# Two attention blocks on one core: block A's projections by quarters of x with all six weight sets for each, and a new written-out loop order

## Chip, core and metric

The kernel runs on one core of a Trainium2 chip. The metric is the device time of one execution in microseconds, as the median of the runs shown. All arithmetic is float32 (the TensorE operands are mostly stored as pairs of a rounded high part and a remainder).

## What is computed

Two attention blocks take inputs of the same shape, x of 2048 x 640, a joint projection weight of 640 x 1920 and an output weight of 640 x 640, with 32 heads of 20. Block A is a local attention: each position looks at 8 positions, itself and every second one before it. Block B is full attention. The outputs stand side by side.

```python
def _A_ref(x, wqkv, wo):
    qkv = (x @ wqkv).reshape(B, S, 3, H, Dh).transpose(2, 0, 3, 1, 4)
    q, k, v = qkv[0], qkv[1], qkv[2]
    idx = pos[:, None] - (jnp.arange(8) * 2)[None, :]      # masked where < 0
    logits = jnp.einsum("bhsd,bhswd->bhsw", q, kg) * scale
    attn = _softmax(jnp.where(mask, logits, -1e9), axis=-1)
    o = jnp.einsum("bhsw,bhswd->bhsd", attn, vg)
    return o.transpose(0, 2, 1, 3).reshape(B, S, D) @ wo
def _B_ref(x, wqkv, wo):
    scores = jnp.einsum("bhqd,bhkd->bhqk", q, k) * (Dh ** -0.5)
    o = jnp.einsum("bhqk,bhkd->bhqd", _softmax(scores, axis=-1), v)
    return o.transpose(0, 2, 1, 3).reshape(B, S, D) @ wo
return jnp.concatenate([_A_ref(...), _B_ref(...)], axis=-1)
```

## The kernel before

**Engines and helpers.** Everything is emitted in program order through a small wrapper (`InOrder`, lines 52 to 66), which is why all instructions of the profile carry line 65. Each engine therefore works through its own list strictly in the order in which the program was written. The profile is read by tile names: `ps_st` is the whole PSUM of eight banks, `w` a tile of a weight set, `akv` a tile of gathered keys or values of block A, `mx` the running maxima of block B, `last` and `big` two pools of larger tiles, `ro` a finished block of 128 x 320 results on its way to memory, `misc` a result of block B on its way to normalization.

**Start.** A short warm-up of TensorE on an identity matrix (lines 216 to 229) comes while the first weights and rows arrive: two transposes and 28 small matmuls in several tile shapes (`in_tiles`). Then come block B's query and key projections (40 groups of 15 matmuls), then its value projection, mixed with the first 80 pairs of matmuls of the maxima pass. From there the main loop runs.

**The main loop** (lines 969 to 1109) follows a written-out order, the string `ORDER`. It is a list of tokens, and the digits behind a letter are the PSUM banks it writes:

- `V`: one of 512 steps of block B's second product (`b_pv`, four matmuls of 128 x 32 by 512, each run as two). A V also begins a new tick (`begin`), on which everything with a due time is issued: DMAs, splits, DVE's pieces of A's softmax.
- `S`, `M`, `Y`: two matmuls of 60 or 62 rows by 512 columns, one on each half of the array's rows. In S both are scores of block B that ScalarE exponentiates. In M both are of the maxima pass, which DVE reduces. A Y has one of each.
- `F`: one step of a projection, two matmuls of 64 rows by 320 columns on the two halves of the array. 30 F tokens make one group of two blocks of 128 x 320.

The work behind F is the list `f_left` (lines 971 to 973): 48 groups of block A's projections (`a_group`), 16 of A's output projection (`oa_group`), 12 of B's (`ob_group`). Groups that `ORDER` doesn't reach are done behind the loop, by `leftover`, with 30 matmuls over all 128 rows instead of 60 over 64.

**A's projections before.** The six weight sets (two of queries, two of keys, two of values, each 640 x 320) pass over x in two halves. `f_left` runs over 12 values of `si`: sets 0 to 5 with the quarters 0 and 1 of x, then the six again with the quarters 2 and 3. Each value has four groups. The first six are loaded raw and split into high part and remainder (`set_pieces`: ScalarE copies, GpSimd subtracts), and the finished tiles are stored to a DRAM tile `w_d`. The second six are read back from it ready-made (`set_again`, two DMAs of 800 KB). A set is asked for at the beginning of the first group of the set before it. The `w` pool holds two sets.

**A's attention** (`a_attention`, with `a_scores`, `a_softmax`, `a_values`) is done by GpSimd on `akv` tiles that DMAs gather from the projected rows in DRAM. It goes by 16 tiles of 128 rows. A tile's scores need its rows of keys, its values its rows of values, and `a_rows` counts both. The function `pump` issues these operations in step with a model of the loop's clock (`COST`, `AHEAD`). Finished tiles are transposed by DVE, pass through DRAM (`a_turn`, `a_back`) and set `ready_a`, without which no group of A's output projection is started.

Of the kernel before, what the change touches and what calls it, by code (L numbers as in the profile page):

```python
# [21 lines left out]
KC = 5  # L22
# [26 lines left out]
NA = 12  # L49
# [20 lines left out]
def attention_pair(ctx, tc, xa, wqk_a, wv_a, wo_a, xb, wqk_b, wv_b, wo_b, oa, ob):  # L70
# [149 lines left out]
    for _ in range(2):  # L220
        pe.transpose(psb[:, 7, :128], ident, ident)

    def in_tiles(rows, cols):
        for r in range(128 // rows):
            for c in range(128 // cols):
                pe.matmul(psb[c * cols:(c + 1) * cols, 5 + r, :128], ident[r * rows:(r + 1) * rows, c * cols:(c + 1) * cols],
                          ident[r * rows:(r + 1) * rows], start=True, stop=True)
    for size in ((64, 128), (64, 32), (64, 128), (64, 32), (64, 128), (128, 32), (64, 128)):
        in_tiles(*size)
# [207 lines left out]
    def normalize(raw, u, then):  # L437
# [15 lines left out]
        t = (1, 4, 5, 8, 10, 11) if then else (1, 5, 6, 10, 12, 14)  # L453
# [57 lines left out]
    def a_softmax(t):  # L511
# [7 lines left out]
        job(soft_jobs, 5, lambda: dve.tensor_reduce(m[:, 0], L.rearrange("p o h -> p h o"), AX.X, ALU.max))  # L519
# [12 lines left out]
        job(soft_jobs, 5, lambda: dve.reciprocal(m[:, 0], m[:, 0]))  # L532
# [23 lines left out]
    def a_attention():  # L556
# [5 lines left out]
        while now[0] < begun + 3:  # L562
            yield False
# [134 lines left out]

    w_d = dr.tile([NA // 2, 2, 128, KC * 320], F32, name="w_d")

# [49 lines left out]
    def xa_pieces(n):  # L750
        def piece(k):
# [3 lines left out]
            after(5, split_piece, k, raw)  # L755
# [215 lines left out]
    f_left = [lambda ns, si=si, n=n, a=a: a_group(si, n, a, ns) for si in range(NA) for n in range(si // 6 * 2, si // 6 * 2 + 2) for a in range(2)]  # L971
# [23 lines left out]
    def pump():  # L995
# [10 lines left out]
        "Y01Y52Y40S36Y41Y35Y72Y60V4Y15S73Y26VY10Y75Y63VY12Y05Y67VY52F01FY36FFFY75FFY32FFFY67FFFFY25FY63VY56FFY73FFF"  # L1006
        "Y25FFY67FFFS32FFFM5FFY73VY61Y25Y37VS12Y06Y53VY61Y23Y70VY36Y51Y27VY03S51Y62VY35Y07Y12VY67Y30Y51VF36Y27FY50FFF"
        "FFY21FFY75FFFY20FFY71VY01Y72VFY75Y12VY05FY12FFY47FFS50FFY21FFFY74FFY05FFFM1V7Y30Y56Y41VY25Y36S04VY26Y31Y50V"
        "Y64S13Y52VY61S02Y43VY65Y13Y02VY41F56FFY02FFY43FFFY10FFY24FFFFM0FS32VY31FY42FFFFY30FFFY41FFY23FFFY40FFM1VY06"
        "Y35Y42VY56Y30S14VY52Y06Y31VM5Y42Y30VY41F65FFY32FFY04FFFY31FFY02FFFY34FFM0VVY04FY23FFFFM0FFY24VY02FFY41FFFY73"  # L1010
        "FFFY40F12FFY37FFFY60FFY45Y37FFFFFY46FFY35Y07V4VY07Y65FFFFFY03FFY76FFFY50FFY73FFFM5VY12Y70Y65VY03Y27Y16VY32"
# [172 lines left out]
```

## Time and profile before

| | |
|---|---|
| median of 3 runs | 1691.92 us (1691.88 to 1693.69) |
| the profiled execution, its own time | 1690.99 us |
| its span, first to last instruction | 1689.2 us |
| PE busy | 1680.1 us (99%) |
| DVE busy | 1360.6 us (81%) |
| ACT busy | 1244.8 us (74%) |
| POOL busy | 938.7 us (56%) |
| DMA, share of the 16 engines' span | 52.6% in the main queue |

PE is TensorE, PEld its weight loads, DVE is VectorE, ACT is ScalarE, POOL is GpSimd, SP is SyncE, which issues nearly all DMAs. The slices of the page cut the span into 40 pieces of 42.2 us, with a digit for the busy tenths of each. Busy times of PE contain matmuls that overlap or wait in the pipeline, so that the 99% don't say how dense the work is; that is read from the starts of successive matmuls.

### The profile page before, as it was taken

Reading aid. Unit: us, or ns where it says so; the run is one execution under the profiler, and the core shown is the slowest. Engines: PE = TensorE matmul, PEld = TensorE weight load, DVE = VectorE, ACT = ScalarE, POOL = GpSimd, SP = SyncE. Lnnn points to the kernel's source line nnn. Section 1 sums busy time; section 2 is a strip of 40 time slices with the busy share of each in tenths; the row PEclk is TensorE's granted clock in tenths of the full one; section 3 lists DMA queues with packets and bytes.
Section 4 is the critical chain, followed back from the end, with each engine's and each line's share of the span. In section 5 each row is a group of like instructions: output and inputs, shape, how many; then the busy total and the mean of one; then the engine's idle time right before and its main releaser. Section 6 shows DMA issues by size and latency. Waiting matters only on the chain.

```text
span 1689.2 us, 37961 instructions
## 1 busy us (share of the span) xinstructions
PE 1680.1 (99%) x14312; PEld 1012.0 (60%) x14312; DVE 1360.6 (81%) x2102; ACT 1244.8 (74%) x2425; POOL 938.7 (56%) x853
## 2 busy tenths in 40 slices
PE   9999999999999999999999999999999999999999
PEld 7888974665655565555565655345454445544669
DVE  4336998998998999899888989889998989888201
ACT  4221158787788778877878788988889888888881
POOL 0000121010179059999999999999999991022420
PEclk9999999999999999999999999999999999999999
DMA  7675553233375355767676765767667652222312
GB/s 252 226 228 175 160 159 108 68 107 101 125 228 164 113 187 189 235 195 223 185 241 187 221 212 159 191 178 214 163 181 191 198 157 72 66 78 67 95 54 90
DMA packets 208071, 272.20 MB, mean 161 GB/s; under 512 B 94860, under 2 KB 126488, under 8 KB 207640
## 3 DMA queue, kind: packets, MB, share of 16 engines
q1 hardware_dynamic: 207252, 269.04, 52.6%
q8 instruction: 112, 1.84, 0.5%
q10 hardware_dynamic: 636, 0.74, 0.1%
q14 instruction: 71, 0.58, 0.1%
HBM read 194.97 MB, written 73.82 MB: 159 GB/s over the span
## 4 chain that ended last, share of the span: by engine, by line
PE 90%; DVE 6%; ACT 1%; POOL 1%; issue 1%; DMA 0%; POOLq 0%; SPq 0%; ACTq 0%; DVEq 0%
PE ps_st L65 90%; DVE mx L65 6%; ACT big L65 1%; POOL akv L65 1%; ACT last L65 0%; DMA akv<-va_d 0%; DVE am L65 0%; ACT misc L65 0%; POOL big L65 0%; POOL misc L65 0%; DVE mxt L65 0%; ACT stg L65 0%; POOL am L65 0%; DVE stg L65 0%; DVE last L65 0%
## 5 line engine op out<-in xcount | busy, mean ns | idle before, releaser
L65 DVE TENSOR_REDUCE mx<-ps_st 128x1 f32<-128x512 f32 (+1 forms) x1811 | 1262.4, 752 | 129.1 <-PE ps_st L65 119.0
L65 ACT ACTIVATE big<-ps_st 128x512 f32<-128x512 f32 x1172 | 636.9, 619 | 130.2 <-PE ps_st L65 117.9
L65 PE MATMUL ps_st<-big,last 60*128 60x512 f32 x2048 | 693.0, 427 | 0.8 <-DVE mx L65 0.2
L65 PE MATMUL ps_st<-last,big 62*128 62x512 f32 x2048 | 666.2, 422 | 3.6 <-ACT big L65 1.2
L65 PEld LDWEIGHTS ps_st<-last,big 62*128 62x128 f32 x2048 | 315.0, 185 | 393.7 <-DVE mx L65 156.0
L65 ACT ACTIVATE last<-ps_st 128x512 f32<-128x512 f32 x876 | 474.5, 621 | 74.8 <-PE ps_st L65 65.7
L65 PE MATMUL ps_st<-w,big 64*128 64x320 f32 (+1 forms) x4560 | 491.1, 307 | 0.0
L65 PEld LDWEIGHTS ps_st<-w,big 64*128 64x128 f32 (+1 forms) x4560 | 427.5, 186 | 33.5 <-issue 6.5
L65 PE MATMUL ps_st<-big,vb 128*32 128x512 f32 x2344 | 384.8, 603 | 0.0
L65 PEld LDWEIGHTS ps_st<-big,last 60*128 60x128 f32 x2048 | 316.9, 184 | 39.1 <-DVE mx L65 19.4
L65 PE MATMUL ps_st<-last,vb 128*32 128x512 f32 x1752 | 307.5, 603 | 0.0
L65 POOL TENSOR_TENSOR akv<-akv 128x640 f32<-128x640 f32 (+3 forms) x304 | 272.4, 934 | 0.0
L65 POOL TENSOR_TENSOR akv<-akv,aq 128x1280 f32<-128x1280 f32 x64 | 187.3, 2949 | 2.3 <-DMA akv<-ka_d 2.3
L65 POOL CAST mtr<-mxt 128x32 fp32r<-128x32 f32 x32 | 6.9, 215 | 312.1 <-DVE mxt L65 311.8
L65 POOL TENSOR_TENSOR akv<-akv,al 128x1280 f32<-128x1280 f32 x64 | 150.5, 2371 | 0.8 <-DMA akv<-va_d 0.7
L65 POOL TENSOR_TENSOR w<-stg,w 128x640 fp32r<-128x640 f32 (+1 forms) x30 | 39.8, 1333 | 150.6 <-ACT w L65 109.3
L65 PEld LDWEIGHTS ps_st<-big,vb 128*32 128x32 f32 x2344 | 60.7, 108 | 100.0 <-issue 94.4
L65 PE MATMUL ps_st<-w,last 64*128 64x320 f32 (+1 forms) x900 | 108.2, 307 | 0.0
L65 PEld LDWEIGHTS ps_st<-last,vb 128*32 128x32 f32 x1752 | 48.4, 108 | 73.2 <-issue 69.1
L65 DVE TENSOR_TENSOR last<-ps_st,last 128x512 fp32r<-128x512 f32 x40 | 27.4, 690 | 78.6 <-ACT last L65 78.6
L65 ACT COPY ro<-ps_st 128x320 f32<-128x320 f32 x154 | 59.1, 438 | 41.1 <-PE ps_st L65 16.6
L65 PEld LDWEIGHTS ps_st<-w,last 64*128 64x128 f32 (+1 forms) x900 | 85.6, 186 | 5.0 <-issue 2.5
(68 smaller groups left out, 797.8 us busy)
## 6 DMA issues: line engine op xcount, KB each, us to landing
akv<-ka_d SPq DMA_DIRECT2D x128, 320.0 KB
akv<-va_d SPq DMA_DIRECT2D x128, 320.0 KB
last<-qb_d SPq DMA_DIRECT2D x128, 160.0 KB
kb_d<-last SPq DMA_DIRECT2D x20, 512.0 KB
qb_d<-last SPq DMA_DIRECT2D x20, 512.0 KB
last<-qb_d SPq DMA_DIRECT2D x128, 80.0 KB
w_d<-w SPq DMA_DIRECT2D x12, 800.0 KB
w<-w_d SPq DMA_DIRECT2D x12, 800.0 KB
```

The lines of the kernel that those rows point to most:

```text
L65: return self.tc.keep_in_program_order(op(*a, **k))
```

## The change

A's projections go by quarters of x. For each of the four quarters all six sets pass, two groups each, so that `f_left` begins with 24 pairs (`u` from 0 to 23, quarter `u // 6`, set `u % 6`). Sets 0 to 5 are loaded raw and split in the first quarter as before. Each of the other three quarters reads all six back from `w_d`: 36 DMAs of 800 KB instead of 12. A set is asked for when the second group of the set two before it has ended, with the pieces one tick apart (raw) or two (read back). The third and the fourth quarter of x are loaded when the first and the second have been used.

The rows of `a_rows` count five ticks after their group instead of three, A's attention begins six ticks after the first rows instead of three, two of its jobs for DVE get a due time of seven instead of five, the splits of x wait eight ticks instead of five, and the last two steps of B's normalization come one tick later.

The warm-up is 19 transposes of the identity instead of two transposes and the small matmuls.

`ORDER` is a new string. Counted by token: F 2070 (2100 before), Y 1544 (1574), S 252 (237), M 172 (157), V 512 (512). One group of 30 F moves behind the loop, where `leftover` finds seven groups instead of six.

```diff
-NA = 12
+NA = 24
...
-    for _ in range(2):
+    for _ in range(19):
         pe.transpose(psb[:, 7, :128], ident, ident)
-
-    def in_tiles(rows, cols):
...
-    for size in ((64, 128), (64, 32), (64, 128), (64, 32), (64, 128), (128, 32), (64, 128)):
-        in_tiles(*size)
...
-        t = (1, 4, 5, 8, 10, 11) if then else (1, 5, 6, 10, 12, 14)
+        t = (1, 4, 5, 8, 10, 11) if then else (1, 5, 6, 10, 13, 15)
...
-        job(soft_jobs, 5, lambda: dve.tensor_reduce(m[:, 0], L.rearrange("p o h -> p h o"), AX.X, ALU.max))
+        job(soft_jobs, 7, lambda: dve.tensor_reduce(m[:, 0], L.rearrange("p o h -> p h o"), AX.X, ALU.max))
...
-        job(soft_jobs, 5, lambda: dve.reciprocal(m[:, 0], m[:, 0]))
+        job(soft_jobs, 7, lambda: dve.reciprocal(m[:, 0], m[:, 0]))
...
-        while now[0] < begun + 3:
+        while now[0] < begun + 6:
...
-    w_d = dr.tile([NA // 2, 2, 128, KC * 320], F32, name="w_d")
+    w_d = dr.tile([6, 2, 128, KC * 320], F32, name="w_d")
...
-            sp.dma_start(AW[si][x].rearrange("p k c -> p (k c)").bitcast(F32), w_d[si - NA // 2, x])
+            sp.dma_start(AW[si][x].rearrange("p k c -> p (k c)").bitcast(F32), w_d[si % 6, x])
...
-            after(5, split_piece, k, raw)
+            after(8, split_piece, k, raw)
...
-    def a_group(si, n, a, ns):
-        assert si in set_in and n in x_in, (si, n)
-        if n % 2 == 0 and a == 0:
-            if si + 1 < NA:
-                spaced(set_pieces(si + 1, 4) if si + 1 < NA // 2 else set_again(si + 1), 1, 3)
-            else:
-                spaced(wide_pieces(wo_a, WO, 0, 4, second=gp), 1, 3)
-        x, W = XA[n], AW[si]
+    def next_set(u):
+        if u < NA:
+            spaced(set_pieces(u, 3) if u < 6 else set_again(u), 1, 1 if u < 6 else 2)
+        elif u == NA:
+            spaced(wide_pieces(wo_a, WO, 0, 4, second=gp), 1, 3)
+
+    def a_group(u, a, ns):
+        n, si = divmod(u, 6)
+        assert u in set_in and n in x_in, (u, now[0] - loop0)
+        if u + a == 0:
+            next_set(1)
+        x, W = XA[n], AW[u]
...
-            if si % 6 in (3, 5):
-                after(3, a_rows.__setitem__, si % 6 // 5, t + 1)
+            if si in (3, 5):
+                after(5, a_rows.__setitem__, si // 5, t + 1)
+        if a:
+            next_set(u + 2)
         if si == 5 and a:
-            spaced(xa_pieces(n + 2), 1, 1)
-        if si == NA - 1 and n == 3 and a:
-            after(1, a_done)
+            if n < 2:
+                spaced(xa_pieces(n + 2), 2, 4)
+            elif n == 3:
+                after(1, a_done)
...
-    f_left = [lambda ns, si=si, n=n, a=a: a_group(si, n, a, ns) for si in range(NA) for n in range(si // 6 * 2, si // 6 * 2 + 2) for a in range(2)]
+    f_left = [lambda ns, u=u, a=a: a_group(u, a, ns) for u in range(NA) for a in range(2)]
...
     ORDER = (
-        "Y01Y52Y40S36Y41Y35Y72Y60V4Y15S73Y26VY10Y75Y63VY12Y05Y67VY52F01FY36FFFY75FFY32FFFY67FFFFY25FY63VY56FFY73FFF"
...
+        "S10Y24Y05Y12Y46Y50Y31Y72V4Y50Y36Y71VY20S53Y76VM0Y62S35VY76F01Y23FFFY57FFY62FFFY35FFY67FFFFY32M5VY32FFFY65FF"
...
```

More of the change, by code (lines that the diff above doesn't have):

```diff
@@ L219, in attention_pair @@
                      pattern=[[-1, 128]], channel_multiplier=1)
-    for _ in range(2):
+    for _ in range(19):
         pe.transpose(psb[:, 7, :128], ident, ident)
-    def in_tiles(rows, cols):
[L224 to L227, printed above, removed]
-    for size in ((64, 128), (64, 32), (64, 128), (64, 32), (64, 128), (128, 32), (64, 128)):
-        in_tiles(*size)
     sel = ident.rearrange("p (j c) -> p j c", j=GH)
@@ L1005, in attention_pair @@
     ORDER = (
-        "Y01Y52Y40S36Y41Y35Y72Y60V4Y15S73Y26VY10Y75Y63VY12Y05Y67VY52F01FY36FFFY75FFY32FFFY67FFFFY25FY63VY56FFY73FFF"
[L1007 to L1010, printed above, removed]
@@ new lines, in attention_pair @@
+        "Y37FFFY62FFY35FFFFY72FY63VY75Y31Y20VY61Y37Y25VY06Y73Y12VY76S50Y31VY57Y61S20VY71Y53Y26VY03Y17Y56VY07Y21Y36V"
+        "Y72F10Y53FFFFY76FFY52FFFY37FFFM5FFM2VVY67Y53FFFS42FM6FFFY53FFFY24FFY75FFFF26FFY43FFY71FFFY54Y03FFY71FFFFM4F"
+        "Y03V7Y01FY45FFFFY30FFY14FFFY53FFFM0FFM4VY36Y12VY45Y30Y61VS54Y20Y36VY50Y46Y21VY36Y50Y24VY35F10FFY64FFY52FFF"
+        "Y34FFY65FFFM2FFY64VY25Y36FFFFFY42FFY53FFFY46FFFFM2FY45VY02Y16Y43VY61Y50S24VM5Y31Y20VY54Y26Y31VY24Y30Y56VY14"
+        "S30Y52VY34Y12Y60VF42FY31FS06FFFFY35FFY07FFS61FFS35FFS70V6VS57FFY03FFFY51FFFY73FFY01FFFFFY73Y50VY17S42Y35VY41"
@@ new lines, in attention_pair @@
+        "VY21Y06FFFFFY27FFY01FFFY26FFY70FFFM1Y76S05VY32S17Y65VY13Y05S27VY36Y51Y02VY73Y65Y10VY76Y25Y13VY62Y05Y71VY30"
+        "Y56Y27VY01Y65Y23VY70F65Y12FFFFFY07FY31FFFFFY72FFFM0VVY02FFY71FFFY03FFY27FFFY10FFY32FFFY71Y32Y60Y15VY06Y73M1V"
+        "VY05Y21F76FFFY43Y50FFFY12Y34FFS05FFY13FFFFY04Y25V3Y04Y12FFFFFY05FFY14FFFY50FFM1FFFM4VY62Y70VY65Y41Y27VY61Y04"
+        "Y52VS10Y67Y54VY70Y41Y62VY70F45Y16FFFFY27FFY01FFFY62FFFFY70FY61VY70Y16VY70FFY61FFFY72FFY60FFFY17FFY62FFFM0V"
+        "Y76Y25Y10VY64Y57Y12VS74Y65Y01VM4Y27S61VY24F06FFY17FFY25FFFY14FFY27FFFFFM4M1VVM4FY71FFFY32FFFFFS75M3FFFFFFM1"
@@ new lines, in attention_pair @@
+        "F75FFY04Y36FFFY21FFFY03FFS24FFFY60FY21V3Y01FY64FFFFY02FFY61FFFY04FFFY62FFM0VY75Y24Y06VY17Y42S05VY62Y14Y07VM5"
+        "S41Y02VS61Y57Y04VY61Y52Y40S17M5Y42VS17Y65Y40VY17Y52Y06VS17M4Y20VY61Y47S25VY06Y41S27VY64Y01Y52VY14Y70Y56VY70"
+        "Y54Y12VY05F67FY14FFFY23FFY50FFFFY43FS12FY50FFM3V1VY23FY50FFFFY42FFFY35FFY40FFFY32FFM4VY02Y73Y65VY07Y34Y26V"
+        "Y54Y03Y27VY34F06Y52FFFFY73FFY45FFFY27FFFFM3FY52VY53FY47FFFFY25FFFY34FFY27FFFFM3FY52VY60Y43Y75VY46Y30Y72VY65"
+        "Y03Y74VS52Y60Y73VY20Y54Y36VY20F54FFY73FFY62FFFY70FFY63FFFFY72FY60VY62FY30FFFFM6VVY20Y63FFFY71FFFY02FY63FFF"
@@ new lines, in attention_pair @@
+        "Y36FFFFFFM2M0VV6Y23FFY07FFFY12FFY30FFFY17FFY32FFFM0Y37Y42VY54Y10S37VY42Y10Y35VY71Y24S03VY24Y75Y01VS73Y45Y02V"
+        "Y31Y25Y74VY50Y31Y27VY34Y05S21VY03F75Y42FFFFFY31FFY20FFFY14FFY03FFM1VM3Y10FFFFFFFY21FFY34FFFY20FFFM3Y21S07V"
+        "Y42Y53Y70VY52S31Y74VM3S25M0VVY42Y37F01FFFY65FFY42FY73FFY65FS24FFFY63FFY72V5Y62FFY43FFFY67FFFY24FFY36FFFY27FF"
+        "M3VY17Y02Y63VY24S07Y61VS10Y34Y72VS16Y40Y23VY01S36Y47VY32Y71Y06VY24S31Y70VY63Y20S41VY62Y07S43VY71Y02Y64VS20"
+        "Y13Y67VY03Y27Y14VY20Y37Y61VY24Y07Y63VY47Y26Y10F35FFFFY47FS26FFFY10FFFY24FFFY76Y01V4Y72Y16VY02Y67FFFFFY01FF"
```

135 lines of the change are left out of this document (59 added, 76 removed).

## The prediction, made before the changed kernel was run

> **What bounds the kernel now.** I began with the page: span, busy times, the chain of work that ended last, and the slices.
>
> ```profile
> span 1689.2 us, 37961 instructions
> PE 1680.1 (99%) x14312; PEld 1012.0 (60%) x14312; DVE 1360.6 (81%) x2102; ACT 1244.8 (74%) x2425; POOL 938.7 (56%) x853
> ...
> POOL 0000121010179059999999999999999991022420
> ...
> PE 90%; DVE 6%; ACT 1%; POOL 1%; issue 1%; DMA 0%; POOLq 0%; SPq 0%; ACTq 0%; DVEq 0%
> ```
>
> The reader is to see that nine tenths of the chain are PE, that the rest is mostly DVE, and that POOL, full from slice 17 to 33, carries 1% of it. So what counts is PE's work and what PE loses between its matmuls. The view by stages, cut at the loop's first token and behind its last, gives the two sums to which everything below is added.
>
> ```profile
> 237.60:1640.70 1403.10, 1398.86 (x12236) 764.40 (x12232) 1211.58 (x1935) 1172.14 (x2289) 918.12 (x824) 1.00 0.53 157
> 1640.70:1689.20 48.50, 45.19 (x304) 44.38 (x302) 6.71 (x7) 8.30 (x20) 0.00 (x0) 1.00 0.22 78
> ```
>
> The loop takes 1403.1 us, 2.74 us for each of its 512 V. The columns are PE, PEld, DVE, ACT and POOL. Neither DVE (86%) nor ACT (84%) is full. The timeline of PE shows what a token costs when nothing waits, from start to start.
>
> ```profile
> 1606.63 0.40 PE L65 MATMUL ps_st<-last,big 62*128 62x512 f32 x2
> 1606.86 1.05 PE L65 MATMUL ps_st<-w,big 64*128 64x320 f32 x12
> 1607.75 0.40 PE L65 MATMUL ps_st<-last,big 62*128 62x512 f32 x2
> 1607.99 0.32 PE L65 MATMUL ps_st<-w,big 64*128 64x320 f32 x2
> ...
> 1608.58 0.39 PE L65 MATMUL ps_st<-last,big 62*128 62x512 f32 x2
> 1608.91 1.07 PE L65 MATMUL ps_st<-last,vb 128*32 128x512 f32 x8
> 1609.79 1.04 PE L65 MATMUL ps_st<-big,vb 128*32 128x512 f32 x8
> 1610.76 0.50 PE L65 MATMUL ps_st<-last,big 62*128 62x512 f32 x2
> ...
> 1643.06 1.92 PE L65 MATMUL ps_st<-w,big 128*128 128x320 f32 x12
> 1644.82 0.60 PE L65 MATMUL ps_st<-w,last 128*128 128x320 f32 x3
> 1645.26 0.59 PE L65 MATMUL ps_st<-misc,ident 128*128 128x512 f32 x1
> ```
>
> A pair of 512-column matmuls (S, M or Y) takes 0.23 to 0.24 us. Six F take 0.89 us, so one takes 0.148 and a group of 30 takes 4.44. A V takes 0.88 before another V and 0.97 before anything else, and the step into a V takes 0.33 instead of 0.24. Behind the loop half a group takes 2.20 us, a group 4.40.
>
> **The change part by part.**
>
> *Tokens.* 30 F leave the loop: 30 x 0.148 = 4.44 us less. 30 Y become 15 S and 15 M: the same number of 512-column pairs, so nothing. V followed by V falls from 50 to 48 by count of the two strings, so there are two more runs of V, at 0.09 + 0.09 us each: 0.4 us more. Behind the loop one group is added: 4.40 us. PE has no room to hide it, because the half groups there follow each other without a gap (1643.06 to 1645.26 is all matmuls).
>
> *What PE loses between tokens.* For this I took stretches of 16 V. First comes all of PE, then the matmuls on weight sets alone (their count is twice the F).
>
> ```profile
> 564.00:611.10 47.10, 47.10 (x444) 28.69 (x440) 42.65 (x67) 36.93 (x71) 13.96 (x13) 1.00 0.44 129
> ...
> 1077.10:1111.40 34.30, 33.78 (x240) 12.51 (x236) 28.99 (x48) 34.07 (x70) 31.45 (x32) 1.00 0.62 162
> ...
> 1195.40:1234.30 38.90, 38.90 (x310) 18.29 (x306) 36.83 (x64) 33.30 (x66) 37.20 (x37) 1.00 0.71 188
> 1234.30:1279.40 45.10, 44.95 (x384) 23.37 (x380) 43.41 (x73) 37.41 (x74) 43.09 (x41) 1.00 0.55 160
> ```
>
> ```profile
> 564.00:611.10 47.10, 19.08 (x180) 16.41 (x180) 0.00 (x0) 0.00 (x0) 0.00 (x0) 1.00 0.44 129
> ...
> 1077.10:1111.40 34.30, 0.00 (x0) 0.00 (x0) 0.00 (x0) 0.47 (x1) 0.87 (x1) 1.00 0.62 162
> ...
> 1195.40:1234.30 38.90, 6.38 (x60) 5.67 (x60) 0.00 (x0) 0.00 (x0) 0.00 (x0) 1.00 0.71 188
> 1234.30:1279.40 45.10, 12.94 (x120) 10.80 (x120) 0.00 (x0) 0.00 (x0) 0.00 (x0) 1.00 0.55 160
> ```
>
> From each stretch I take off its F at 0.148 and its pairs at 0.235 (the pairs are all matmuls, less those on weights, less 128 of the V, halved). What remains is 16 V and the lost time: 21.1 us with no F, 20.1 with 30, 20.2 with 60, 17.8 with 90. F tokens dilute the waits for banks, by (21.1 - 17.8) / 90 = 0.037 us each. To the 30 that leave this adds 1.1 us. Spreading the others evenly, which the new order does (seven stretches with 30 F or fewer before, two after), gains nothing as long as these four points lie on a straight line. That is the value I take. If instead only the poor stretches pay, five of them could fall from some 20.6 to 17.8, 14 us less. If the even spread takes from the rich stretches what it gives the poor and the new places of the banks are worse, I allow 8 us more (32 stretches at a quarter of a microsecond, less than a tenth of the distance between the rows).
>
> *Sets by quarters.* The 48 groups of matmuls are the same, and so are the six raw loads and their splits. Added are 24 DMAs that read sets back, 19.7 MB, and the time for them to land is shorter.
>
> ```profile
> q1 hardware_dynamic: 207252, 269.04, 52.6%
> ```
>
> ```profile
> 591.82 0.34 SPq L65 DMA_DIRECT2D w<-w_d  x1
> ...
> 604.62 0.34 SPq L65 DMA_DIRECT2D w<-w_d  x1
> ```
>
> SP spends 0.34 us on such an issue, 8 us on 24, and PE doesn't wait for it. The main queue moved 269 MB in 52.6% of the span, 3.3 us of all 16 engines for each MB, so 19.7 MB take 65 us of DMA time. They fall into some 255 V (700 us) of the loop, which makes the DMA share there about 0.09 higher. The issues of one set stood 12.8 us apart where the program asks for three ticks, 8.2 us: SP's queue was 4.6 us late. What is queued behind a read-back on SP are the fetches of `akv`, the q and k loads and the stores. It waits there until PE has left the set's tiles, one tick after the group's end, so for a few us. Before, a set had 16 to 28 V from the request to its first use (counted in the string). After, it has 14 to 30, and at the shortest (sets 5, 6 and 17) 14 or 15, 38 us. Two ticks between the parts, 5.5 us, the queue's lateness of 4.6, and 1.6 MB at the 65 us / 19.7 MB above, 5.4 us alone or three times that in a busy stretch, make 16 to 27 us. I take nothing. The upper end is a rival.
>
> *A's attention.* The first line is SP's fetches of `akv` (least, median and greatest ns of an issue, first and last start), the second POOL's longest operation on them.
>
> ```profile
> L65 SPq DMA_DIRECT2D akv<-ka_d x128: 319/422/1962, 463.5 to 1304.2; - x128
> ```
>
> ```profile
> L65 POOL TENSOR_TENSOR akv<-akv,aq 128x1280 f32<-128x1280 f32 x64 | 187.3, 2949 | 2.3 <-DMA akv<-ka_d 2.3
> ```
>
> The first keys are stored after group 6 instead of 12, V 50 instead of 75, so with the longer waits POOL begins near V 61, 405 us by 237.6 + 61 x 2.74, instead of 463. The work itself does not change:
>
> ```profile
> 550.00:600.00 50.00, 0.00 (x0) 0.00 (x0) 0.00 (x0) 0.00 (x0) 3.94 (x2) 1.00 0.39 123
> ...
> 650.00:1380.00 730.00, 0.00 (x0) 0.00 (x0) 0.00 (x0) 0.00 (x0) 612.08 (x469) 1.00 0.67 197
> ```
>
> This is POOL on `akv` alone: near idle for 50 us for lack of values, then 730 us without a pause. 612 us are 0.84 of that stretch. With the rest of its work POOL needs some 50 us for a tile, 200 for a quarter, and quarters are complete at V 82, 161, 242 and 333, 80 to 90 V or 220 to 250 us apart. So POOL will pause before each quarter. The last values come at V 333, near 1150 us, and with some 2.5 tiles' work left POOL ends near 1275 instead of after 1380. The output projection of A begins at V 350 instead of 304 and ends at 472 instead of 466, so nothing that PE does comes sooner. I cost the earlier attention at nothing, and its cover is that PE had F to do all the time in both orders. POOL's splits of sets 4 and 5 and of two quarters of x now queue among attention operations of up to 2.95 us. The longer due times (five to eight, five to seven, three to five ticks) are 5 to 8 us for that.
>
> *Warm-up.* It ends at 6.69 now, and PE runs without a gap from there. The first three real matmuls start 0.48 us apart, later ones about 0.23.
>
> ```profile
> 1.36 0.48 PE L65 MATMUL ps_st<-ident 128*128 128x128 f32 x1 [1.36 <-POOL ident L65]
> ...
> 1.36 0.69 PE L65 MATMUL ps_st<-ident 128*128 128x128 f32 x2 [1.36 <-POOL ident L65]
> ...
> 5.27 0.62 ACT L65 CAST big<-last 128x512 fp32r<-128x512 f32 x1 [1.09 <-DMA last<-xb]
> ...
> 6.69 9.64 PE L65 MATMUL ps_st<-big 128*128 128x512 f32 x38
> ```
>
> ```profile
> L65 PE MATMUL ps_st<-big 128*128 128x512 f32 x3 | 1.6, 683 | 0.0
> ...
> L65 PE MATMUL ps_st<-big 128*128 128x512 f32 x20 | 4.7, 389 | 0.0
> ```
>
> The last two are groups of PE alone, from 6.69 to 8.13 us (three starts in 1.44 us) and from 12 to 16. One transpose ends after 0.48 us, two after 0.69, so 19 take between 0.48 + 18 x 0.21 = 4.3 and 19 x 0.34 = 6.5 us. The first real matmul needs the cast that ends at 5.89, so it would start between 5.9 and 7.9 instead of at 6.69: -0.8 to +1.2, and I take 0. That matmuls go at half pace until about 8.1 us I read as a clock that is not yet full, though the granted clock stands at 1.00 in every window of the trace. [...]
>
> *The sum:* 1690.99 - 4.44 + 0.4 + 4.40 + 1.1 = 1692.5 us for a profiled execution. The median of the runs lies 0.93 above the profiled one, so the forecast is **1693.4 us**, 0.09% above before. A measurement of this kernel can tell about 0.2%, 3.4 us, from no change.
>
> **The rivals.**
>
> 1. *Late weight sets: slower.* The reading back waits behind SP's queue and lands after PE wants it. It decides where request to landing exceeds 38 us. For it: SP's 4.6 us, POOL's splits among attention work, a lead that shrinks to 14 V. Against it: 16 to 27 us by the sum above, and POOL's 64 first operations on fetched keys waited 2.3 us for DMAs in all. If seven sets (those with leads up to 16 V) come 1.5 us late, 1693.4 + 10.5 = 1704. Chance 0.15.
> 2. *The warm-up warms nothing: slower.* Now the slow matmuls end 6.8 us after the first warm-up instruction (1.36 to 8.1). If the count begins with the first real matmul near 6.5, they end near 13.3, 5.2 us later, at half speed: +2.6 us, 1696. The granted clock of the windows says nothing for or against it. Chance 0.1.
> 3. *The new order's own waits are worse: slower.* The 8 us above: 1701. For it: stretches of 16 V with 90 F or more, the cheapest, fall from ten to five. Chance 0.11.
> 4. *The straight line is bent: faster.* Only poor stretches pay, and the even spread recovers half of the 14 us: 1686.4. For it: in the stretch without F, ACT is busy for 34.07 of 34.30 us. Against it: 20.1, 20.2 and 21.1 at 30, 60 and 0 F. Chance 0.22.
>
> That A's attention doesn't begin sooner at all would leave the sum as it is, since it is costed at nothing.
>
> **How the numbers follow.** Forecast 0.42; slower 0.15 + 0.1 + 0.11 = 0.36; faster 0.22. The forecast's own range is 1690 to 1695. The range reaches over the rivals to 1685 below and 1704 above and leaves out the ends of the first and the fourth, and what several at once would make.
>
> **What the profile will show.** Right: PE's share stays at 99%; the loop is 2 to 4 us shorter and the part behind it 4.4 longer; `w<-w_d` stands at 36; POOL begins near 405 and has pauses before the later quarters; the DMA share in the middle is near 0.75. The first rival would show as PE waiting for DMAs on `w` or for POOL's `w`, the second as more than three slow matmuls behind the warm-up, the third and the fourth as the loop's time alone, with PEld's waits for DVE `mx` and ACT up or down. A loop changed by over 8 us with none of these waits would make the prediction wrong in its central step, the straight line.

## The result, and the profile after

| | before | after |
|---|---|---|
| median of the runs beside each other | 1692.62 us (1691.88 to 1693.69, 4 runs) | 1705.66 us (1705.34 to 1707.84, 4 runs) |
| ratio | | 1.0078, 95% interval 1.0066 to 1.0090 |
| span of the profiled execution | 1689.2 us | 1703.5 us |

The kernel is 0.8% slower. The forecast was 1693.4 us with a range of 1685 to 1704, so the time lies just above the range's upper end. The page of the changed kernel hardly shows it:

```profile
span 1703.5 us, 37844 instructions
PE 1687.9 (99%) x14243; PEld 1015.9 (60%) x14243; DVE 1362.6 (80%) x2087; ACT 1245.9 (73%) x2425; POOL 938.0 (55%) x853
...
POOL 0000121205999249999479998389899961121520
...
PE 85%; DVE 5%; POOL 3%; DMA 2%; issue 2%; ACT 1%; SPq 1%; ACTq 0%; POOLq 0%; DVEq 0%
```

PE's share stays at 99%, and POOL now begins earlier and has three pauses. The last line, the chain of work that ended last, is the one that changed: PE falls from 90% to 85%, while POOL rises to 3% and DMA to 2%, where they had 1% and 0%. The view by stages tells where the time is. The first row is the loop, the second what lies behind it, the third a stretch inside the loop; the column behind POOL is PE's granted clock.

```profile
236.90:1650.70 1413.80, 1403.61 (x12177) 763.61 (x12173) 1213.40 (x1920) 1172.52 (x2287) 917.45 (x824) 1.00 0.56 170
1650.70:1703.50 52.80, 49.44 (x332) 48.70 (x332) 6.71 (x7) 9.04 (x22) 0.00 (x0) 0.99 0.22 79
1364.50:1371.30 6.80, 5.23 (x24) 2.07 (x28) 5.05 (x9) 2.86 (x6) 6.25 (x5) 0.50 0.78 239
```

The loop begins 0.7 us sooner (236.9 for 237.6), and the part behind it is 4.3 us longer (52.8 for 48.5; 4.4 were predicted). The loop takes 1413.8 us, 10.7 more than before, where 2.9 less were predicted (1403.1 - 4.44 + 0.4 + 1.1 = 1400.2). **The miss is 13.6 us, all of it inside the loop.** The third row is a part of it: for 6.8 us PE's clock is at half.

Just ahead of that stretch the timeline of the changed kernel (start, length, engine, operation, and in brackets the idle time before it and what ended it) shows PE, DVE and POOL like this:

```profile
1360.22 3.19 POOL L65 TENSOR_TENSOR ao<-ao,akv 128x640 f32<-128x640 f32 x2
1363.36 0.46 POOL L65 TENSOR_TENSOR am<-al 128x128 f32<-128x128 f32 x1
1363.90 0.65 POOL L65 TENSOR_TENSOR am<-am 128x64 f32<-128x64 f32 x2
...
1361.78 0.65 DVE L65 TENSOR_REDUCE mx<-ps_st 128x1 f32<-128x512 f32 x1
1364.58 0.35 DVE L65 RECIPROCAL am<-am 128x32 f32<-128x32 f32 x1 [2.15 <-POOL am L65]
1364.85 1.75 DVE L65 TENSOR_REDUCE mx<-ps_st 128x2 f32<-128x1024 f32 x2
...
1362.91 0.50 PE L65 MATMUL ps_st<-big,last 60*128 60x512 f32 x1
1366.07 0.79 PE L65 MATMUL ps_st<-last,big 62*128 62x512 f32 x1 [2.65 <-DVE mx L65]
```

DVE works in order. Its reciprocal of A's softmax waits 2.15 us for POOL's sums, and the maxima of block B wait behind it. PE gets no bank back and stands 3 us between the starts at 1362.91 and 1366.07. Its next matmul takes 0.79 us instead of 0.40. In the kernel before, the timeline shows the same place without a wait, but with nothing to spare: the sums end at 1373.33 (1372.67 + 0.66), and the reciprocal starts at 1373.36.

```profile
1372.13 0.47 POOL L65 TENSOR_TENSOR am<-al 128x128 f32<-128x128 f32 x1
1372.67 0.66 POOL L65 TENSOR_TENSOR am<-am 128x64 f32<-128x64 f32 x2
...
1373.36 0.35 DVE L65 RECIPROCAL am<-am 128x32 f32<-128x32 f32 x1
```

A second group of losses lies between 1136 and 1221 us, where A's output weights (`wo_a`) are loaded and split. In the kernel before, the six loads start between 997.6 and 1067.9 us, in the changed one between 1130.9 and 1201.8. These are SP, ACT and PE there, in the timeline of the changed kernel:

```profile
1129.20 0.80 SPq L65 DMA_DIRECT2D va_d<-ro  x2
1130.09 0.75 SPq L65 DMA_DIRECT2D big<-kb_d  x2
1130.89 0.36 SPq L65 DMA_DIRECT2D stg<-wo_a  x1
...
1133.51 2.93 SPq L65 DMA_DIRECT2D mdr<-mtr  x4
...
1140.72 0.56 SPq L65 DMA_DIRECT2D sm<-misc  x1
1141.33 0.55 SPq L65 DMA_DIRECT2D last<-qb_d  x1
1143.69 0.34 SPq L65 DMA_DIRECT2D stg<-wo_a  x1
...
1148.62 0.73 ACT L65 CAST w<-stg 128x640 fp32r<-128x640 f32 x1 [1.24 <-DMA stg<-wo_a]
...
1149.90 0.49 PE L65 MATMUL ps_st<-big,last 60*128 60x512 f32 x1 [1.26 <-ACT big L65]
```

From 1129 on SP has a burst of DMAs: stores of values, keys and queries of the next unit of block B, maxima, a normalization, A's fetches and now `wo_a` too. ACT, in order as well, waits for a load of `wo_a`, its exponentials come late, and PE waits for them. In the table of waits over the whole changed kernel this is one row, which the profile of the kernel before does not have (microseconds, times, longest):

```profile
ACT w L65 <- DMA stg<-wo_a: 4.2, 3, 2.3
```

### The profile page after: what moved, and what is told of

It is laid out like the page before. It is cut to its first block, busy times and chain, and to the rows that moved or that the text cites. A ratio compares the mean times of both kernels' runs of the same rounds, so it can differ in the third digit from the quotient of the medians.

```text
span 1703.5 us, 37844 instructions
## 1 busy us (share of the span) xinstructions
PE 1687.9 (99%) x14243; PEld 1015.9 (60%) x14243; DVE 1362.6 (80%) x2087; ACT 1245.9 (73%) x2425; POOL 938.0 (55%) x853
## 4 chain that ended last, share of the span: by engine, by line
PE 85%; DVE 5%; POOL 3%; DMA 2%; issue 2%; ACT 1%; SPq 1%; ACTq 0%; POOLq 0%; DVEq 0%
PE ps_st L65 85%; DVE mx L65 5%; POOL akv L65 2%; DMA akv<-va_d 1%; SPq L65 1%; ACT big L65 1%; DMA stg<-wo_a 1%; ACT last L65 0%; POOL ao L65 0%; DMA last<-xb 0%; POOL big L65 0%; POOL am L65 0%; DMA big<-kb_d 0%; POOL al L65 0%; DVE am L65 0%
## 5 line engine op out<-in xcount | busy, mean ns | idle before, releaser
L65 POOL TENSOR_TENSOR big<-stg,big 128x512 fp32r<-128x512 f32 (+1 forms) x40 | 55.9, 1397 | 76.6 <-ACT big L65 54.7
```

The costliest lines, as they stand in the source:

```text
L65: return self.tc.keep_in_program_order(op(*a, **k))
```

## The experiments

My first theory (T1 in the expectations) made one story of both: the raw buffers (`stg`) come free late, SP stops, ScalarE waits for `wo_a`, GpSimd falls behind, and the stall at 1364 us is the end of it.

| run | what | total, us | loop, us | half clock in the loop, us |
|---|---|---|---|---|
| before | | 1692.6 | 1403.1 | 0 |
| after | | 1705.7 | 1413.8 | 6.8 |
| e1_stg4 | fourth raw buffer | 1708.1 | 1415.9 | 13.6 |
| e2_wo84 | later split, first half | 1705.2 | 1413.5 | 10.2 |
| e3_hold | GpSimd gets 10 us | 1700.3 | 1408.7 | 0 |
| e5_wodve | splits on DVE | 1710.6 | 1418.9 | 13.6 |
| e6_pause | pause, never reached | 1707.4 | 1416.1 | 10.2 |
| e7_before_lag | before, GpSimd late | 1694.8 | 1406.5 | 0 |
| n_before | before, no attention of A | 1688.5 | 1399.9 | 3.4 |
| n_after | after, no attention of A | 1690.9 | 1399.0 | 3.4 |
| e8_pause2 | pause at the last tile | 1702.2 | 1410.8 | 3.4 |
| e9_after_nosplit | e8, no splits of wo_a | 1699.7 | 1408.2 | 3.4 |
| e9_before_nosplit | before, no splits of wo_a | 1697.8 | 1408.3 | 3.4 |
| e10_double | e8, more DMA | 1706.6 | 1415.1 | 6.8 |
| e11_late9 | e8, wo_a loaded later | 1701.6 | 1408.3 | 3.4 |
| e12_late9_stg4 | e11 and fourth buffer | 1700.7 | 1406.7 | 0 |
| w_before_newwarm | before, new warm-up | 1692.2 | 1406.1 | 3.4 |

The totals of before, after, e8, e12 and w_before are medians of 4 to 10 executions, the others single ones. The loop is that of one profiled execution, from the start of its first token to the end of its last; the last column is the length of the stretches in it with a granted clock of 0.5. I take a stretch of 3.4 us at half clock as a cost of up to 1.7, half its length; that is an estimate from the granted clock of 0.50 (in one of them PE does 16 matmuls in the time of 28, see the last section). Whether there is one near 240 us changes from execution to execution (e11 has one from 242.6 us, e12 none there), so loops are compared after taking that off. Totals of single executions of one kernel lie up to 3 us apart (before: 1691.4 to 1694.7 in 13 runs), and the profiled execution of the kernel before, 1690.99 us, is 1.6 faster than its median, so a difference of 1 to 2 us between single loops shows little by itself.

Where the order of PE's work is the same in two runs, I also set the n-th matmul of one loop beside the n-th of the other and read how far one has fallen behind. That shows, to a few tenths of a microsecond, in which stretch a difference arises.

### What T1 got right and wrong

**e1_stg4**

```diff
-    def stg(tag="stg", bufs=3):
+    def stg(tag="stg", bufs=4):
...
-        r = sb.tile([128, 320], F32, tag="r", bufs=4, name="ro")
+        r = sb.tile([128, 320], F32, tag="r", bufs=2, name="ro")
```

> The changed kernel with a fourth raw buffer of the kind that wo_a's pieces, a_turn and a_back share (the room comes from two of the four ro buffers). Order of all instructions unchanged. Theory T1 (the last quarter's attention on GpSimd falls together with the splits of wo_a; the shared raw buffers come free late, SP stops, ScalarE waits in order for wo_a, GpSimd falls behind, and at 1364 us DVE waits for GpSimd, PE stands idle and loses its clock): ScalarE's waits for wo_a fall from 4.2 us to under 1.5, SP's silence from 1190.9 to 1199.1 goes, and the loop falls from 1413.8 us to 1402 to 1406. Rival R1 (SP is late there because of the number of transfers queued, not because of buffers): ScalarE's waits stay at 3 us or more, the loop within 3 us of 1413.8. Rival R2 (GpSimd's lag at 1364 doesn't come from wo_a at all): the waits at 1140 to 1210 go, the stall at 1364 stays, loop 1407 to 1410.

ACT's waits for `wo_a` fell from 4.2 us to 1.7, but DVE waited 2.17 us at 1364 as before, and the loop, less 6.8 us for half clock, has 1409.1 us where the changed kernel has 1410.4. (As measured, 1415.9 us, the loop fits only R1, whose long waits of ACT are not there.) So SP's wait for a raw buffer is a small part at most, and the stall at 1364 does not come from these waits.

**e2_wo84**

```diff
-            spaced(wide_pieces(wo_a, WO, 0, 4, second=gp), 1, 3)
+            spaced(wide_pieces(wo_a, WO, 0, 8, second=gp), 1, 3)
```

> The changed kernel with the split of wo_a's first half eight ticks behind its load instead of four; the second half as it was. T1: the first half's wait of ScalarE (1.24 us at 1148.6) and PE's stall of 1.4 us at 1150 go, the second half's waits (3.0 us) and the stall at 1364 stay: loop 1411 to 1413. R3 (the due time was simply too short and everything later follows from that first wait): stall and clock dip at 1364 go too, loop 1403 to 1406.

The loop is within what T1 allowed once the new half clock near 1214 us is taken off, but the reason isn't T1's: all of ACT's waits for `wo_a` went, those for the second half too, and DVE still waited 2.17 us at 1364. From e2's timeline:

```profile
1364.25 0.35 DVE L65 RECIPROCAL am<-am 128x32 f32<-128x32 f32 x1 [2.17 <-POOL am L65]
```

It is the same wait in the changed kernel, in e1 and in e2, with ACT waiting 4.2, 1.7 and 0 us for `wo_a`. So the stall at 1364 does not grow out of these waits: T1's chain breaks there, and R3, which made everything later follow from the first of them, fails too. The stalls of PE at 1148 and 1206 are gone in e2, although the loads still lie in SP's burst: from 1145 to 1213 us PE gains 3.4 us on the changed kernel. Then it waits 0.96 us for GpSimd's part of a turned tile, the clock falls, and most of the gain is lost again.

**e3_hold**

```diff
     def a_done():
+        after(20, hold)          # hold(): gp.us += 10
```

> The changed kernel with 10 us more put on the clock by which GpSimd's attention is issued, once, 20 ticks after A's last projection: GpSimd gets 10 us to catch up before the stretch at 1364. T1: the waits between 1136 and 1221 stay (4.2 us on ScalarE), but DVE's wait of 2.15 us for GpSimd, PE's stall of 3 us and the half clock behind it go: loop 1406 to 1409. R4 (the dip of the clock at 1364 has nothing to do with GpSimd): dip stays, loop 1412 to 1416.

As T1 expected, DVE's wait fell to 0.35 us, the clock stayed full, and the loop fell by 5.1 us to 1408.7:

```profile
1373.04 0.35 DVE L65 RECIPROCAL am<-am 128x32 f32<-128x32 f32 x1 [0.35 <-POOL am L65]
```

Set beside the changed kernel matmul by matmul, 3.9 of the 5.1 us are won between 1360 and 1380, the rest before (ACT's waits for `wo_a` are 2.8 us here, not the 4.2 that T1 expected to stay). So the stall at 1364 with its half clock is some 4 us of the loss, and it is GpSimd being late at that place.

**e5_wodve**

```diff
-wide_pieces(wo_a, WO, 0, 4, second=gp)
+wide_pieces(wo_a, WO, 0, 4)
```

(the same for the second half)

> The changed kernel with the remainder of wo_a's splits (six subtractions, 7.9 us) made by DVE instead of GpSimd. T1: raw buffers come free sooner and GpSimd has 8 us less work and two waits fewer, so the stall at 1364 goes; DVE takes some 4 us more within 80 us, of which PE may feel 1 to 2: loop 1403 to 1408. R2: stall at 1364 stays, loop 1411 to 1416.

A miss: DVE now waits for ACT's casts of `wo_a` there (4.5 us in four waits), and PE for DVE. The stall at 1364 shrank (DVE waited 0.65 us), but PE lost more between 1140 and 1206, and 10.2 us at half clock follow, 1207 to 1217. With 7.9 us less to do, GpSimd is less late at 1364; but PE, too, is 9 us later there than in the changed kernel, so the run doesn't tell which of the two made the wait shorter.

### The stall at 1364 us

Why does GpSimd's lateness count at just this place, when e1 and e2 leave it as it was? The reciprocal is a job with a due time of seven ticks. But where a tile's values begin, `aside` brings the rest of its softmax to an end at once. For all tiles but the last, scores of later tiles lie between sum and reciprocal. Behind the last tile there are none: both are issued in the same tick, in both kernels, and the due time never acts. DVE then waits for whatever GpSimd is late. The traces agree: in the kernel before, the reciprocals of the other 15 tiles start 1.05 us or more behind the end of their sums, the last one 0.03. In the changed kernel two more have lost their distance (0.09 us at 516.7 and 0.15 at 999.5), though DVE doesn't wait there. Why GpSimd is some 2 us later at the last tile than before, no run shows.

**e6_pause** and **e8_pause2** put two ticks between them. In e6 the pause stood behind a step that had already run, so it was never reached, and the run is one more execution of the changed kernel's order (DVE waited 2.12 us).

> The changed kernel with one pause of two ticks in GpSimd's attention, between the sum of the last tile's softmax and its reciprocal on DVE. The runs so far put DVE's wait of 2.15 us, PE's stall of 3 us and the half clock behind it down to this place: the last tile has no scores of a later tile behind it, so its sum (GpSimd) and its reciprocal (DVE) are issued in the same tick, and whatever GpSimd is late by then, DVE and PE wait for. If that is right, the stall goes without the 10 us that the earlier run gave: loop 1407 to 1409, total 5 to 6 us below the changed kernel. If the 10 us mattered in another way (less work of GpSimd beside wo_a), the loop stays within 2 us of 1413.8.

```diff
             aside(t, c)
+            if c == 4:
+                until = now[0] + 2 * (t == NT - 1)
+                while now[0] < until:
+                    yield False
+                for _ in soft.pop(t):
+                    run_jobs(soft_jobs, 1)
```

(e8; the last two lines move here out of `aside`)

> The changed kernel with two ticks between the last tile's sum (GpSimd) and its reciprocal (DVE), this time put ahead of the place where the softmax of that tile is brought to its end: the earlier run's pause stood behind the sum's own step and was never reached. If the sum and the reciprocal in one tick are the cause of the stall at 1364: DVE's wait of 2.15 us, PE's stall of 3 us and the half clock go, loop 1406 to 1409 (from 1413.8), 5 to 7 us less in all, about 1699 to 1701. If not: loop 1412 to 1416.

The timeline of e8 shows the reciprocal without a wait:

```profile
1369.96 0.34 DVE L65 RECIPROCAL am<-am 128x32 f32<-128x32 f32 x1
```

and its stages a loop of 1410.8 us, with one stretch at half clock that belongs to the stall at 1148:

```profile
237.10:1647.90 1410.80, 1402.70 (x12177) 763.90 (x12173) 1212.95 (x1920) 1170.93 (x2287) 918.02 (x824) 1.00 0.56 170
1151.40:1154.80 3.40, 3.40 (x23) 2.86 (x19) 1.27 (x3) 2.29 (x5) 3.40 (x3) 0.51 0.99 348
```

Less 1.7 us for that, 1409.1: the same as e3, a little over the range that I gave. Between 1360 and 1380 e8 gains 4.5 us on the changed kernel, matmul by matmul. Over four executions e8 stands at 1.0051 of the kernel before (1.0034 to 1.0068), where the changed kernel has 1.0078 (1.0066 to 1.0090).

**e7_before_lag** makes GpSimd late in the kernel before.

```diff
-        pool(m, L[:, :4], L[:, 4:], ALU.add)
+        for _ in range(7 if t == NT - 1 else 1):
+            pool(m, L[:, :4], L[:, 4:], ALU.add)
```

> The kernel before with the first of the last tile's three sums done seven times (six more operations of 0.46 us on GpSimd, 2.8 us, same result), so that GpSimd is late at this place by as much as in the changed kernel. In the kernel before, DVE's reciprocal there doesn't wait. If lateness at this one place costs what it seems to: DVE waits about 2 us, PE stalls about 3, the granted clock falls to half for some 7 us, and the total rises by 5 to 7 us over before. If the clock's fall needs something else of the changed kernel: the total rises by 0 to 3 us and the clock stays.

From its timeline:

```profile
1372.90 3.67 POOL L65 TENSOR_TENSOR am<-al 128x128 f32<-128x128 f32 x7
...
1377.33 0.35 DVE L65 RECIPROCAL am<-am 128x32 f32<-128x32 f32 x1 [3.25 <-POOL am L65]
...
1378.28 0.50 PE L65 MATMUL ps_st<-big,last 60*128 60x512 f32 x1 [2.33 <-DVE mx L65]
```

The wait can be made at will, and the loop grew by 3.4 us, 3.0 of them between 1370 and 1380; the total, 1694.8, is 2.1 over the median of the kernel before. The clock did not fall (1.00 from 1375 to 1383 us), which is the second of the two cases. So the place is a weak spot that the kernel before has too; there GpSimd was not late enough to show it.

### The orders by themselves

**n_before, n_after**

```diff
     def a_attention():
+        return
...
-    next_back, ready_a, f_done = [0], [0], [0]
+    next_back, ready_a, f_done = [0], [NT], [0]
```

(and the tiles of A's output projection are set to zero)

> The kernel before without A's attention: GpSimd does none of it, no tile is turned or fetched, and A's output projection reads zeros. Loads and splits of weights, the projections and all of block B stay, and so does the order of the matmuls. Its loop, beside that of the next run, shows what the two orders cost by themselves. Loop 1385 to 1398 (from 1403.1).

> The changed kernel without A's attention, as in the run before. If the new order by itself is as dense as the old one (the straight line of the prediction), the loop is 2 to 4 us shorter than that of the kernel before without attention. If the new order's own places of the banks are worse (the third rival), it is 2 us or more longer. If it's neither, the cost of the change lies in its meeting with A's attention.

The loops, n_before and then n_after:

```profile
238.40:1638.30 1399.90, 1396.90 (x12237) 763.44 (x12233) 1187.20 (x1823) 1159.50 (x2257) 144.61 (x168) 1.00 0.29 86
```

```profile
237.30:1636.30 1399.00, 1395.41 (x12177) 758.68 (x12173) 1188.64 (x1808) 1157.07 (x2255) 144.11 (x168) 1.00 0.33 100
```

Both have 3.4 us at half clock. Without A's attention the new order is 0.9 us shorter, not the 2.9 of the sum, and nowhere near the third rival's 8 us more. With A's attention it is 10.7 longer. The cost of the change lies in the meeting of the new order with A's attention, almost all of it. Attention here means also its DMAs: without it the DMA share falls from 0.53 to 0.29 and from 0.56 to 0.33.

Set beside each other matmul by matmul, the runs with and without attention show where. From 260 us to 1145 the kernel before falls 3.8 us behind n_before, the changed kernel 4.3 behind n_after: up to there attention costs both orders nearly the same. Behind 1145 us the first loses 0.9 more, the second 12.0.

### The stalls between 1136 and 1221 us

**e9_after_nosplit, e9_before_nosplit** fill A's output weights without a split.

```diff
             w = W[half]
+            if src is wo_a:
+                for x in range(2):
+                    sp.dma_start(w[x][:, a:b].bitcast(F32), w_d[5, x].rearrange("p (k c) -> p k c", k=KC)[:, a:b])
+                if b == KC:
+                    after(wait, w_in.add, id(w[0]))
+                return
```

> The run before, and in addition A's output weights not split: their tiles are filled by DMAs from a ready-made set (set 5 of the projections, so A's output is another), without raw buffers, ScalarE's six casts (4.0 us) and GpSimd's six subtractions. If the splits of wo_a beside the last quarter's attention cost what the waits of PE in the stretch 1136 to 1221 show (1.4 + 1.0 + 1.2 us, and some smaller ones), the loop falls by 4 to 6 us below that of the run before, to 1401 to 1404. If these waits are the order's own, by 0 to 2 us.

> The kernel before without the split of wo_a, in the same way. There the same splits lie at 998 to 1078 us, with GpSimd as full. If their place in the changed kernel is the worse one, the loop falls by less here than there: 0 to 2 us, to 1401 to 1403. If they cost as much here, the move explains nothing: 4 us or more.

Less its half clock, the first has 1406.5 us, 2.6 under e8: between the two cases. The second has 1406.6 instead of 1403.1, longer without the split than with it, which neither case allowed; I have no explanation for that, so the pair does not price the move of the splits. What it did show is that a stall at 1148 doesn't need the splits. In the timeline of the first, with no cast of `wo_a` left:

```profile
1144.15 0.62 SPq L65 DMA_DIRECT2D sm<-misc  x1
...
1151.32 0.25 DVE L65 RECIPROCAL sm<-sm 128x16 f32<-128x16 f32 x1 [2.80 <-DMA sm<-misc]
...
1152.17 0.50 PE L65 MATMUL ps_st<-last,big 62*128 62x512 f32 x1 [1.93 <-DVE mx L65]
```

Now it is DVE that waits, in block B's normalization, for a load that SP issued at 1144.15 instead of 1140.72. PE is only 1.5 us later at this place than in the changed kernel, so SP is some 1.9 us further behind, and whoever is due first waits for it.

The kernel before can show such a stall as well. In w_before_newwarm (below), which has its loop, PE stops for 1.68 us beside its loads of `wo_a`, behind a load of a turned tile (`tr_d`):

```profile
1067.34 0.72 ACT L65 CAST big<-stg 128x640 fp32r<-128x640 f32 x1 [1.19 <-DMA stg<-tr_d]
1069.10 0.49 PE L65 MATMUL ps_st<-last,big 62*128 62x512 f32 x1 [1.68 <-ACT big L65]
```

So the changed kernel did not bring in this kind of stall.

**e10_double** adds DMA traffic.

```diff
             sp.dma_start(AW[si][x].rearrange("p k c -> p (k c)").bitcast(F32), w_d[si % 6, x])
+            sp.dma_start(w_x[si, x], w_d[si % 6, x])
```

> The changed kernel with the two-tick pause and each of the 36 DMAs that read a set back followed by a second of the same size from memory to memory on the same queue (29.5 MB more than in the run before, 1.5 times what the change added). If what is left of the loss is the load on the DMA queues or on SP (the first rival), the loop rises by 4 us or more over the run with the pause alone; if the sets read back cost nothing, it stays within 1.5 us.

The loop rose by 4.3 us, 1.7 of it a stretch at half clock. As measured that is just over the 4 us that I had set for the first case; without the half clock it lies between the two. PE waited for no weight set. The largest part of the rest is a new stall of PE of 2 us at 1002. In the timeline:

```profile
1003.25 0.59 ACT L65 COPY misc<-ps_st 128x512 f32<-128x512 f32 x1 [3.12 <-POOL misc L65]
...
1003.88 0.50 PE L65 MATMUL ps_st<-big,last 60*128 60x512 f32 x1 [1.94 <-ACT misc L65]
```

ACT's copy of a result of block B waits for GpSimd's multiplication of the one before. DVE also waits there, 4.12 us for A's sums at 1006.0, and 1.12 us at 519.0, at tiles that are not the last. So more traffic does cost something, through a GpSimd that comes late, and the due times don't cover it. By proportion the change's own traffic, two thirds of this, would cost (4.3 - 1.7) x 2/3 = 1.7 us; that is an estimate, and too low if anything, because e8's stall of 1.94 us at 1148, with its half clock, is one of 0.79 us without in e10. But the added reads are not what is left of the loss. The changed kernel issues its last `w<-w_d` at 1110.8 us, and up to 1145 the two orders lose nearly the same to attention (above).

**e11_late9, e12_late9_stg4** go behind SP's burst.

```diff
-            spaced(wide_pieces(wo_a, WO, 0, 4, second=gp), 1, 3)
+            spaced(wide_pieces(wo_a, WO, 0, 4, second=gp), 10, 3)
```

> The changed kernel with the two-tick pause, and the three loads of wo_a's first half asked for nine ticks later, behind the burst of DMAs that SP issues around the 320th V (1129 to 1149 us). If SP's lateness in that burst is what stalls PE at 1148 (1.4 to 2.1 us in the runs so far, with a half clock of 3.4 us behind it in one of them): the stall goes, the one at 1206 stays, loop 1406 to 1408.5. If the stall at 1148 is the order's own: 1408 to 1411 and the stall is there.

> The run before with the fourth raw buffer as well (for two of the ro buffers). If SP's wait of 8 us for a raw buffer at 1191 to 1199 makes the stall at 1206: that goes too, loop 1405 to 1407, total 1697 to 1699, which leaves 4 to 6 us of the loss unexplained by any single stall. If the raw buffers don't matter: as the run before, 1 us or less apart.

In both, ACT's waits for `wo_a` are gone altogether (4.5 us in e8), and so are the stalls of PE at 1148 and 1206. Less half clock, e11's loop has 1406.6 us, 2.5 under e8. This is e12's:

```profile
236.90:1643.60 1406.70, 1400.66 (x12177) 762.86 (x12173) 1212.38 (x1920) 1170.45 (x2287) 917.00 (x824) 1.00 0.56 171
```

So moving three loads by nine ticks took away both stalls, and the buffer adds nothing. By e2 a later split alone does it too: the split came too soon for a load that late. The size, 2.5 us, is one of single loops. Over four executions each, e12 and e8 are hardly apart: e12 stands at 1.0052 (1.0037 to 1.0067) of the kernel before, e8 at 1.0051, with medians of 1700.7 (1697 to 1699 were expected) and 1702.2 us. No complete version of the new order that I ran beats the kernel before.

### The warm-up

**w_before_newwarm**

```diff
-    for _ in range(2):
+    for _ in range(19):
         pe.transpose(psb[:, 7, :128], ident, ident)
```

(and without the small matmuls)

> The kernel before with the changed kernel's warm-up alone (19 transposes for two transposes and 28 small matmuls). If transposes warm the clock as matmuls do, the loop begins some 0.5 to 1 us sooner (237.6 before) and the total falls by as much, less than can be told. If they don't (the second rival), the first matmuls go at half pace until 13 us and the loop begins 2 to 3 us later.

The loop begins at 236.5 us instead of 237.6, and the total is 0.9997 (0.9987 to 1.0006) of the kernel before: no difference that can be told. The profile's record of the granted clock begins, at full, at 4.2 us in this run, at 8.2 in the kernel before and at 6.0 in the changed kernel; where there is no record the windows show 1.00, so the 1.00 that the prediction read in them is no measurement for the first 8.2 us.

## Why the prediction was wrong

**What held.** The group behind the loop cost 4.3 us (4.4). The profile has 36 DMAs `w<-w_d`, no engine waits for them, and the main queue moved 288.7 MB for 269.0, the 19.7 that were worked out: no late weight sets. The straight line is off by 2 us, the difference between 0.9 and 2.9 in the runs without A's attention. Its slope, 0.037 us for each F, rests on four stretches. Another of 16 V with 90 F in the kernel before, 753.7 to 804.0 us, leaves 19.9 by the same sum where the one shown leaves 17.8; over all its stretches of 16 V the slope is about 0.021, which makes 0.6 us of the 1.1.

**Warm-up.** I took 0 out of -0.8 to +1.2 for the first real matmul; it starts 0.46 us sooner, and the loop 0.7. The timeline of the changed kernel:

```profile
1.36 4.32 PE L65 MATMUL ps_st<-ident 128*128 128x128 f32 x19 [1.36 <-POOL ident L65]
6.23 10.07 PE L65 MATMUL ps_st<-big 128*128 128x512 f32 x42 [0.55 <-ACT big L65]
```

42 real matmuls take 10.07 us, 0.24 each. Only the first two starts are 0.34 us apart and those that follow 0.23, but for 0.37 and 0.34 behind 8.84 and 9.21 us; the kernel before had 0.59, 0.43, 0.43 and 0.28 and needed 9.64 us for 38. The second rival is refuted, for these float32 transposes. Its 6.8 us from the first warm-up instruction to the end of the slow matmuls are the kernel before's alone; in the changed kernel the starts are 0.23 us apart from 6.57 us on, 5.2 behind that instruction.

**The step that failed** is the one that says "I cost the earlier attention at nothing, and its cover is that PE had F to do all the time in both orders." PE had F to do. But its tokens stand in a fixed order, and it waits for the banks that DVE and ACT give back (2.65 us for DVE's `mx` at 1366.07, 1.26 for ACT's `big` at 1149.90). Those two work in order as well, with pieces of A's attention and splits of A's weights among their work on block B. So an operation of A that comes late stops block B, however much F there is. By the prediction's own sign, a loop changed by over 8 us with none of the rivals' waits, the straight line would be the step that failed; the runs without attention speak against that, as it is off by 2 us of the 13.6.

Two sizes of it are shown. At the last tile, sum and reciprocal in one tick: 4.7 us with the half clock (1413.8 to e8's 1409.1). The prediction counted on "the longer due times" as cover; at this place they never act, which could have been read from `aside`. And the loads of `wo_a`, moved into a burst of SP's: about 2.5 us (e8 to e11, single loops). The prediction counted SP's lateness, 4.6 us, for the sets that are read back; that the loads of `wo_a` move, and what else stands in the queue where they come to lie, it did not look at.

With the 2 us of the orders this makes 9.2 of 13.6 us. **The other 4.4 stay open.** They come up only with A's attention: e12 has 3.6 us more than the kernel before, n_after 0.9 less than n_before. Matmul by matmul the place can be seen. From 260 to 1200 us e12 loses 4.1 us to n_after, the kernel before 3.9 to n_before. From 1200 to 1340 e12 loses 4.0 more, the kernel before 0.3. In that stretch A's output projection runs beside the end of A's attention. It does so in the kernel before as well, so the reason stays open. PE's longest idle time in e12's loop is 0.96 us, at 1213.6, for GpSimd's part of a turned tile, the first that A's output projection needs; the rest is in shorter waits.

**A's attention does begin sooner and gains nothing by it.** I gave 405 us for its beginning and 1275 for its end. From the view of the tile `akv` on POOL in the changed kernel (least, median and greatest ns; first and last start):

```profile
L65 POOL TENSOR_TENSOR akv<-akv,aq x64: 2920/2940/3002, 402.6 to 1300.4; 128x1280 f32<-128x1280 f32 x64
...
L65 POOL TENSOR_TENSOR ao<-ao,akv x48: 1543/1562/1612, 501.8 to 1390.3; 128x640 f32<-128x640 f32 x48
```

In the kernel before:

```profile
L65 POOL TENSOR_TENSOR akv<-akv,aq x64: 2917/2946/2989, 472.9 to 1316.3; 128x1280 f32<-128x1280 f32 x64
...
L65 POOL TENSOR_TENSOR ao<-ao,akv x48: 1545/1562/1592, 632.5 to 1395.0; 128x640 f32<-128x640 f32 x48
```

It starts 70 us sooner and ends 5 us sooner. The pauses before each quarter give the time back, as predicted in kind. The estimate of "2.5 tiles' work left" when the last values come, near 1150 us, was far too low: 240 us are nearly five tiles at the prediction's own 50. So GpSimd is nearly as full as before when A's weights and turned tiles come (busy for 222 of the 240 us from 1150 to 1390, before 232), and behind 1145 us lie the waits.

**The rivals.** The first gave the nearest time (1704), but PE waited for no set that was read back; only its premise, a late queue on SP, came up, at the loads of `wo_a`. The third (1701) also has the wrong mechanism: the order's own waits are not it. Of the fourth, that poor stretches would gain 7 us, nothing shows in the 0.9 us between n_before and n_after.

## What to carry to other kernels

A due time protects an engine only where something stands between the two operations, and only from a lateness shorter than that: look at the last round of a pipelined sequence, where the work that kept them apart has run out. When a block of work is moved, read what each in-order queue, that of the DMAs above all, already holds at the new place. And run both orders without the work that goes on beside them: that tells in two runs whether an order is worse or only what it meets. Set beside the full runs matmul by matmul, they also tell where.

## What was not expected of the hardware

The granted clock fell to 0.50 within the loop in 13 of the 17 runs of the table, in the changed kernel in a loop with PE busy for 1403.61 of 1413.80 us, and behind the same stall it fell in one run and not in another. At the loop's start PE stalls 0.81 us in e12 and in n_after alike. These are the stages of e12 there:

```profile
237.00:240.40 3.40, 2.15 (x14) 0.92 (x11) 2.50 (x4) 3.16 (x7) 0.00 (x0) 1.00 0.60 222
240.40:243.80 3.40, 3.40 (x28) 1.40 (x28) 3.40 (x7) 3.11 (x8) 0.00 (x0) 1.00 0.95 269
```

and of n_after:

```profile
237.40:240.80 3.40, 2.17 (x14) 0.89 (x10) 2.50 (x4) 3.12 (x7) 0.00 (x0) 0.99 0.60 224
240.80:244.20 3.40, 3.40 (x16) 1.09 (x16) 2.83 (x5) 2.26 (x5) 0.00 (x0) 0.50 1.00 267
```

PE was busy 2.15 and 2.17 us of 3.40, and then n_after does 16 matmuls in the time in which e12 does 28. All such stretches in the loops lasted 3.4, 6.8 or 10.2 us. In n_after the clock fell behind 3.40 us in which PE was busy for 2.17, with no idle time longer than 0.81 us, and it did not fall behind one of 2.33 us in e7, where PE was busy for less of the time:

```profile
1375.00:1379.00 4.00, 1.67 (x14) 0.79 (x6) 1.67 (x5) 1.65 (x4) 3.10 (x7) 1.00 0.00 0
1379.00:1383.00 4.00, 4.00 (x31) 1.34 (x29) 3.67 (x10) 3.41 (x7) 4.00 (x2) 1.00 0.21 39
```

In the 17 runs of the table, PE's busy share in the 3.4 us ahead of a fall was 0.35 to 0.66 for 16 of the 19 falls in loops (0.60 ahead of the one at 1364.5 us in the changed kernel), and 0.87 for three at the start of the old order's loop. Without a fall it was 0.63 in e12 (2.15 of 3.40) and 0.42 in e7 (1.67 of 4.00). What decides is left open.
